# Linear attention into a Swish layer: fewer idle products at the start, beta copied earlier, batch 2's numerators moved

## The chip, the cores and the metric

The kernel runs on one core of a Trainium2 chip. Its five engines work side by side, each through its own queue of instructions in order: PE (TensorE, matrix products; its weight loads are listed as PEld), DVE (VectorE), ACT (ScalarE), POOL (GpSimd) and SP (SyncE, which here issues DMAs only). They wait for one another through semaphores. The metric is device time in microseconds (us), the median of the runs. Line numbers (L254) are those of the kernel before.

## The reference

Inputs: q, k, v of shape 8 x 8 x 576 x 64 (batch, heads, positions, head size), w_in 512 x 2048, w_out 2048 x 512, beta 2048, all float32.

```python
def phi(x): return np.where(x > 0, x, np.exp(x) - 1.0) + 1.0
q_p, k_p = phi(q), phi(k)
kv  = np.einsum('bhsd,bhse->bhde', k_p, v)
z   = np.sum(k_p, axis=2)
num = np.einsum('bhsd,bhde->bhse', q_p, kv)
den = np.einsum('bhsd,bhd->bhs', q_p, z)[..., None] + 1e-06
x   = num / den          # then to (8*576) x 512, heads side by side
h   = x @ w_in
g   = h * (1.0 / (1.0 + np.exp(-beta * h)))
out = g @ w_out
```

So each batch goes through a small attention part (phi, kv, z, numerators) and then through two large products, of 512 by 2048 and back.

## The kernel before, in words

Everything is written in the order in which it is to be queued; nothing is rearranged later, so the order of the lines is the order of work on each engine. Large data is bf16, sums are float32 in PSUM.

**Tiling.** A batch has 576 positions: four blocks of 128 and a tail of 64, called t = 0 to 4. The tails of all batches are collected in xT_tail and done as a ninth batch at the end. The two big products of a batch are h_phase (16 groups, one for each ff, of four products 128 x 128 by 512; `h_mm`, L331, then Silu on ACT) and y_phase (four tiles y of sixteen products; `y_mm`, L349, then `y_out`). The attention part of batch b + 1 is put between these groups: `at(sh, n, f)` runs f behind group n of h_phase, `at(sy, n, f)` behind group n of y_phase. Their instructions go into the same PE queue, so a product that must wait holds all groups behind it.

**Start.** For batch 0 there is no other work to hide in. `idle(n)` (L130) queues n products that nobody reads. Then come, on PE: the transposes of phi_q (`q_trans`, L254, 16 of them into two PSUM tiles tps), three idle products, z's products (L187) of head pair 0, six idle products, z's of pair 1, kv's products of pair 0 (`kv_direct`), the denominators (`dens`, L411), two groups of numerators of pair 0 (`numer_part`, L490), kv's of pair 1. phi itself is an exponential on ACT (`phi_part`, L141), a relu on DVE (`phi_relu`, L145, called r) and a minimum of both on DVE (`phi_min`, L152). Of kv, pair 0 goes from PSUM into kv0 by two masked DVE operations, pair 1 by four casts on ACT (L543), which numer_part(..., 1) needs. beta is loaded as a row, turned by one product into bps (L538) and copied by ACT into beta_s (L546). The numerators, divided, are xs; `x_part(t, pr)` transposes a half of xs on PE (L511) and copies it with ACT (L515) into xT, and `h0_part` (L521) makes the first h products, block by block.

The PSUM tiles of `q_trans`, bps and x_part share a pool of two buffers, in turn: a tile waits until the tile two places before it has been read. bps and x_part(0, 0) take the two buffers, so x_part(1, 0) waits for the copy of bps.

**Batch 2 inside batch 1.** During h_phase of batch 1: phi_q of batch 2 is transposed by two DMAs issued on SP, `q_trans_dma` (L265), one for each half of the partitions, into qTd; `kv_both` (L176) stands behind group 6; x_trans(1, 4) behind group 8; and `numer(2, t)` (L282) behind groups 9, 11, 13, 15 and 16, that is, the first group of y_phase for the last one. A numer makes four products, two with the first half of qTd and two with the second, then three DVE operations (L290, L291, L296). Its PSUM tile has a pool of one buffer. One group later `x_trans_dma` (L323) transposes the xs by a DMA on SP. For the later batches the numerators lie behind groups 5, 7, 9, 11 and 13.

phi_q of batch 2 is worked on DVE behind the last copies of xT and y_sb of the phase before. v of batch 2 comes through POOL's DMA queue and is copied by POOL itself into vaug (`v_copy`, L166). The loads of q and k for batch 3 wait for qTd by an explicit dependency (`hold`).

Of the kernel before, what the change touches and what calls it, by code (L numbers as in the profile page):

```python
# [8 lines left out]
F32 = mybir.dt.float32  # L9
# [7 lines left out]
def kernel(  # L17
# [10 lines left out]
    nc = tc.nc  # L28
# [4 lines left out]
    P = 128  # L33
    KC = DM // P
    FC = DFF // P
# [10 lines left out]
    miscps = ctx.enter_context(tc.tile_pool(name="miscps", bufs=2, space=bass.MemoryType.PSUM))  # L46
# [44 lines left out]
    beta_row = consts.tile([FC, P], F32)  # L91
# [10 lines left out]
    ident16 = consts.tile([FC, FC], F32)  # L102
# [25 lines left out]
    def idle(n, cols=512):  # L128
        for _ in range(n):
            nc.tensor.matmul(  # L130
                warm_ps[:, 0:cols], warm[:, 0:P], warm[:, 0:cols], start=True, stop=True
            )
# [31 lines left out]
    def v_copy(eng, b, pr):  # L164
        src = vb[b % 2] if b == 2 else vf[b % 2]
        eng.tensor_copy(  # L166
            vaug[b % 2][:, pr, :, :, 0:D],
            src[:, 2 * pr : 2 * pr + 2].rearrange("p h j d -> p j h d"),
        )
# [13 lines left out]
    def row_products(b, pr, dsts, mov):  # L183
        for j in range(J):
            for hh in range(2):
                r = slice(hh * G, (hh + 1) * G)
                nc.tensor.matmul(  # L187
                    dsts[hh], st[b, "k"][r, pr, j, :], mov(r, j),
                    start=(j == 0), stop=(j == J - 1), skip_group_check=True,
                )  # L190

    def z_products(b, pr, ps):

        row_products(b, pr, [a[:, 256 + 2 * pr : 258 + 2 * pr] for a in ps], lambda r, j: ones[r])

    def z_evac(ps):
        for hh in range(2):
            nc.vector.tensor_mul(
                z0[:, hh], ps[hh][:, 256:260].rearrange("p (a h) -> p a h", a=2),
                kvmask[:, :, :, 0],  # L200
            )

    def kv_direct(b, pr, ps):
        row_products(
            b, pr, [a[:, pr * P : (pr + 1) * P].rearrange("p (h d) -> p h d", h=2) for a in ps],
            lambda r, j: vb[b][r, 2 * pr : 2 * pr + 2, j, :],
        )
# [53 lines left out]
    def q_trans_dma(b):  # L261
        st[b, "qTd"] = work.tile([P, 38, G], BF16, tag="qT", name="qTd")
        nc.gpsimd.memset(st[b, "qTd"][:, 36:37], 0.0)
        for hh in range(2):
            st[b, "qTd", "dma"] = nc.sync.dma_start_transpose(  # L265
                out=st[b, "qTd"][:, hh * 2 * J : (hh + 1) * 2 * J],
                in_=st[b, "q"][hh * G : (hh + 1) * G].rearrange("p a j c -> p (a j c)"),
            )

    def q_stat(b, t, hh, pr, n):  # L270
        if (b, "qTd") in st:
            i = (hh * 2 + pr) * J + 2 * t
            return st[b, "qTd"][:, i : i + 2, :].rearrange("p j g -> p (j g)")
        return st[b, "qT"][:, t, pr, hh, 0:n]
# [32 lines left out]
    def x_trans(b, t, eng):  # L307
        n = P if t < NT - 1 else G
        xv = st[b, "xs", t].rearrange("p i a d -> p (i a d)")
        tp = miscps.tile([P, KC, P], BF16, tag="misc", name="xtp")  # L310
        for p in range(KC):
            nc.tensor.matmul(  # L312
                tp[:, p, :n], xv[:n, p * P : (p + 1) * P], identity[:n, :n],
                is_transpose=True, start=True, stop=True, skip_group_check=True,
            )
        if eng is nc.scalar:
            nc.scalar.copy(x_dst(b, t), tp[:, :, :n])
        else:
            eng.tensor_copy(x_dst(b, t), tp[:, :, :n])  # L319
# [23 lines left out]
    def mm_tile(name):  # L343
        return mmps.tile([P, 512], F32, tag="mm", name=name)
# [45 lines left out]
    beta_s = consts.tile([P, FC], F32)  # L390
# [10 lines left out]
    def misc_bf():  # L401
        return miscps.tile([P, 1024], BF16, tag="misc", name="tp")
# [18 lines left out]
    def num0_tile():  # L421
        return num0ps.tile([P, 512], F32, tag="num0", name="nps0")
# [16 lines left out]
    def phi_step(a, pr, f, *r):  # L439
        f(0, a, pr, *((xin(0, a, pr),) if f is not phi_min else ()), *r)  # L440
# [5 lines left out]
    phi_step("q", 0, phi_part)  # L446
    phi_step("q", 1, phi_part, 0, 4)
    phi_step("q", 1, phi_part, 4, J)
    idle(20)
    phi_step("q", 0, phi_relu)  # L450
    phi_step("q", 0, phi_min)
    phi_step("q", 1, phi_relu)
# [24 lines left out]
    z_products(0, 0, zt)  # L477
    idle(6)
    z_products(0, 1, zt)
    z_evac(zt)  # L480

    def q_trans0(t):
# [2 lines left out]
    def numer_part(ts, pr):  # L485

        nps = num0_tile()
        for i, t in enumerate(ts):
            for hh in range(2):
                nc.tensor.matmul(  # L490
                    nps[:, (i * 2 + hh) * P : (i * 2 + hh + 1) * P].rearrange(
                        "p (h d) -> p h d", h=2
                    ),
                    q_stat(0, t, hh, pr, P),
                    st[0, "kv"][:, hh, pr, :].rearrange("p (h e) -> p h e", h=2)[:, :, 0:D],
                    start=True, stop=True, skip_group_check=True,
                )
        for i, t in enumerate(ts):
            if pr == 0:
                st[0, "xs", t] = work.tile([P, 4, 2, D], BF16, tag="xs", name="xs", bufs=4)  # L500
            nc.vector.tensor_mul(  # L501
                st[0, "xs", t][:, 2 * pr : 2 * pr + 2].rearrange("p i a d -> p a i d"),
                nps[:, i * 256 : (i + 1) * 256].rearrange("p (a h d) -> p a h d", a=2, h=2),
                rden0[:, t, :, 2 * pr : 2 * pr + 2, None].to_broadcast([P, 2, 2, D]),
            )

    def x_part(t, pr):
        xv = st[0, "xs", t].rearrange("p i a d -> p (i a d)")
        tp = misc_bf()[:, 0:256].rearrange("p (c t) -> p c t", c=2)
        for c in range(2):  # L510
            nc.tensor.matmul(  # L511
                tp[:, c], xv[:, (2 * pr + c) * P : (2 * pr + c + 1) * P], identity,
                is_transpose=True, start=True, stop=True, skip_group_check=True,
            )
        nc.scalar.copy(xT[0][:, 2 * pr : 2 * pr + 2, t * P : (t + 1) * P], tp)  # L515

    def h0_part(t, pr, ffs=range(4)):

        for ff in ffs:
            for kc in range(2 * pr, 2 * pr + 2):  # L520
                nc.tensor.matmul(  # L521
                    hps[ff][:, t * P : (t + 1) * P],
                    w_in_sb[0][:, kc, ff * P : (ff + 1) * P],
                    xT[0][:, kc, t * P : (t + 1) * P],
                    start=(t == 0 and kc == 0), stop=(t == 3 and kc == KC - 1),
                    skip_group_check=True,
                )
# [6 lines left out]
    numer_part((0, 1), 0)  # L534
    numer_part((2, 3), 0)
    kv_direct(0, 1, kvp0)
    bps = miscps.tile([P, FC], F32, tag="misc", name="bps")
    nc.tensor.matmul(bps, beta_row, ident16, is_transpose=True, start=True, stop=True)  # L538

    for hh in range(2):  # L540
        for h in range(2):
            r = slice(h * D, (h + 1) * D)
            nc.scalar.copy(  # L543
                kv0[r, hh, 1, h * EA : h * EA + D], kvp0[hh][r, P + h * D : P + (h + 1) * D]
            )
    nc.scalar.copy(beta_s, bps)  # L546
    hps = [mm_tile("h_ps") for _ in range(4)]
    x_part(0, 0)
    x_part(1, 0)
    numer_part((0, 1), 1)  # L550
    h0_part(0, 0)
    x_part(2, 0)
    h0_part(1, 0)
    x_part(3, 0)
# [138 lines left out]
    def at(side, n, *fs):  # L693
        side.setdefault(n, []).extend(fs)


    for b in range(1, B + 1):
        n = b + 1
        sh, sy = {}, {}
        if b == 1:  # L700
            at(sh, 0, lambda: q_trans_dma(2))
            at(sh, 8, lambda: x_trans(1, 4, nc.vector))
            at(sh, 1, lambda: [v_copy(nc.gpsimd, 2, pr) for pr in range(2)])
            at(sh, 2, lambda: load_kq(3, st[2, "qTd", "dma"]), lambda: load_v(3))
        if n < B:
            at(sh, 6 if b == 1 else 4, lambda: kv_both(n))
            for t in range(NT):
                ff = min((9 if b == 1 else 5) + 2 * t, FC)
                for g, f in ((ff, numer), (ff + 1, x_trans_dma)):
                    at(*((sh, g) if g < FC else (sy, g - FC)), lambda t=t, f=f: f(n, t))  # L710
        if n + 1 < B:
            m = n + 1
            at(sy, 0, lambda: phi_all(m, "q"))
            at(sy, 2, lambda: q_trans_dma(m), lambda: load_kq(m + 1, st[m, "qTd", "dma"]))
            at(sy, 6, lambda: phi_all(m, "k"), lambda: [v_copy(nc.gpsimd, m, pr) for pr in range(2)])
            at(sy, 7, lambda: load_v(m + 1))
        h_phase(b, xT[b % 3] if b < B else xT_tail, sh)
        y_phase(b, sy, last=(b == B))
# [30 lines left out]
```

## Time and profile before

| | us |
|---|---|
| median of 3 runs (294.74 to 295.0) | 294.87 |
| the profiled execution, its own time | 295.34 |
| its span, first to last instruction | 293.6 |
| PE busy | 286.4 |
| ACT busy | 160.2 |
| DVE busy | 115.9 |
| first h product of 512 columns (L331) starts | 21.19 |
| h_phase of batch 1 starts | 52.68 |

Times in the profile count from the start of the span. Timelines have one line for a run of like instructions: start, length, engine, line, operation, what it writes and reads, how many, and in brackets the idle time before it on its engine and what ended it. The chain of waits is the work that ended last, followed back from the end: each piece is what the next one waited for. An end of a PE product is modelled, so starts are the safer numbers.

The granted clock of TensorE reads 1.00 in every stretch.

### The profile page before, as it was taken

What the parts mean: (1) busy time and instruction counts of PE and PEld (TensorE: products, weight loads), DVE (VectorE), ACT (ScalarE), POOL (GpSimd) and SP (SyncE); (2) the same over time, 40 slices, a digit from 0 to 9 for tenths busy, and PEclk for the clock granted to TensorE, in tenths of its full rate; (3) what the DMA queues carried; (4) which work ended last, traced back from release to release, by engine and by line L of the source; (5) the groups of instructions that cost most, each with busy time, mean ns of one, the idle gap of its engine ahead of it and who ended that gap; (6) DMA issues with size and microseconds to landing.
All of it is one profiled execution on the core that took longest, in us unless ns stands there. A gap on an engine that the chain in (4) does not pass through costs nothing.

```text
span 293.6 us, 4773 instructions
## 1 busy us (share of the span) xinstructions
PE 286.4 (98%) x1890; PEld 143.8 (49%) x1890; DVE 115.9 (39%) x267; ACT 160.2 (55%) x217; POOL 36.9 (13%) x54
## 2 busy tenths in 40 slices
PE   8989999999999999999999999999999999999994
PEld 2674457454445444544455445544554444444443
DVE  5742776843815461446135613562251200110021
ACT  5677757957635862677267815790660077017500
POOL 8632100220050005000500053000000000000000
PEclk9999999999999999999999999999999999999999
DMA  8999999699799859953997399728132310130032
GB/s 217 206 227 387 261 232 178 129 224 189 94 166 286 132 71 194 281 86 55 181 285 107 44 197 264 116 42 157 38 72 45 74 36 0 43 84 18 0 74 73
DMA packets 50887, 40.83 MB, mean 139 GB/s; under 512 B 30752, under 2 KB 42288, under 8 KB 50864
## 3 DMA queue, kind: packets, MB, share of 16 engines
q1 hardware_dynamic: 37968, 23.48, 37.9%
q0 software_dynamic: 12736, 16.91, 30.0%
q8 instruction: 15, 0.25, 0.3%
q10 hardware_dynamic: 160, 0.13, 0.2%
q14 instruction: 8, 0.07, 0.1%
HBM read 36.71 MB, written 9.44 MB: 157 GB/s over the span
## 4 chain that ended last, share of the span: by engine, by line
PE 96%; DVE 2%; ACT 1%; issue 0%; DVEq 0%
PE y_ps L349 42%; PE h_ps L331 42%; PE warm_ps L130 3%; PE nps L282 2%; PE kvp L176 2%; PE h_ps L521 1%; PE kv L187 1%; PE xtp L312 0%; PE nps L429 0%; PE nps L254 0%; PE tp L511 0%; PE nps L411 0%; DVE xs L501 0%; DVE phi_k L152 0%; DVE xs L296 0%
## 5 line engine op out<-in xcount | busy, mean ns | idle before, releaser
L339 ACT ACTIVATE g<-h_ps,beta_c 128x512 bf16<-128x512 f32 x144 | 98.0, 688 | 100.5 <-PE h_ps L331 100.0
L349 PE MATMUL y_ps<-w_out,g 128*128 128x512 bf16 (+3 forms) x600 | 127.2, 370 | 0.0
L331 PE MATMUL h_ps<-xT,w_in 128*128 128x512 bf16 x496 | 114.7, 379 | 0.3 <-DVE xT L319 0.2
L349 PEld LDWEIGHTS <-g 128*128 128x128 bf16 x600 | 58.0, 98 | 64.7
L331 PEld LDWEIGHTS <-w_in 128*128 128x128 bf16 x560 | 52.7, 98 | 57.8 <-issue 0.2
L234 DVE COPY y_sb<-y_ps 128x512 f32<-128x512 f32 (+2 forms) x35 | 23.4, 673 | 84.7 <-PE y_ps L349 81.0
L296 DVE TENSOR_TENSOR xs<-nps,rden 128x512 bf16<-128x512 f32 (+1 forms) x36 | 24.7, 689 | 5.9 <-DMA xT<-xs 3.5
L82 POOL DMA_DIRECT2D xq<-in_q_dram x7 | 5.2, 744 | 109.6 <-DMA qTd<-phi_q 105.9
L141 ACT ACTIVATE e<-xk 128x1152 bf16<-128x1152 bf16 x16 | 17.9, 1153 | 1.0 <-DMA xk<-in_k_dram 0.9
L152 DVE TENSOR_TENSOR phi_q<-e,r 128x1152 bf16<-128x1152 bf16 (+2 forms) x17 | 12.0, 720 | 14.0 <-ACT e L141 13.7
L141 ACT ACTIVATE e<-xq 128x1152 bf16<-128x1152 bf16 x14 | 15.6, 1156 | 0.1
L331 PE MATMUL h_ps<-xT_tail,w_in 128*128 128x512 bf16 x64 | 14.0, 379 | 0.0
L226 DVE TENSOR_TENSOR kv_bd<-kvp,kvmask 128x260 bf16<-128x260 f32 x12 | 4.6, 423 | 23.7 <-PE kvp L176 23.7
L290 DVE TENSOR_SCALAR den<-nps 128x8 f32<-128x8 f32 (+1 forms) x30 | 4.9, 165 | 22.7 <-PE nps L282 22.7
L282 PEld LDWEIGHTS <-qTd 128*128 128x128 bf16 x120 | 9.3, 98 | 7.7 <-DVE xs L296 0.9
L152 DVE TENSOR_TENSOR phi_k<-e,r 128x1152 bf16<-128x1152 bf16 x16 | 11.6, 753 | 2.2 <-ACT e L141 2.0
L282 PE MATMUL nps<-kv_bd,qTd 128*128 128x130 bf16 x120 | 11.9, 221 | 0.4 <-DVE xs L296 0.4
L166 POOL CAST vaug<-vf 128x1152 bf16<-128x1152 f32 x10 | 11.2, 1157 | 5.1 <-DMA vf<-in_v_dram 5.1
L130 PE MATMUL warm_ps<-xT 128*128 128x512 bf16 x29 | 9.7, 500 | 1.5 <-DVE xT L95 1.5
L141 ACT ACT_TABLE_LOAD x6 | 7.7, 1283 | 2.0 <-DMA xq<-in_q_dram 1.2
L339 ACT ACT_TABLE_LOAD x6 | 7.7, 1283 | 0.1
L176 PEld LDWEIGHTS <-phi_k 64*128 64x128 bf16 x216 | 6.3, 94 | 2.5 <-issue 2.1
(81 smaller groups left out, 122.1 us busy)
## 6 DMA issues: line engine op xcount, KB each, us to landing
out_dram<-y_sb SPq DMA_DIRECT2D x70, 128.0 KB, 2.4
vf<-in_v_dram SPq DMA_DIRECT2D x5, 1152.0 KB, 10.2
xk<-in_k_dram POOLq DMA_DIRECT2D x7, 576.0 KB, 13.9
xq<-in_q_dram POOLq DMA_DIRECT2D x7, 576.0 KB, 8.9
w_in<-in_moe_w_in_dram POOLq DMA_DIRECT2D x4, 512.0 KB, 12.4
g<-in_moe_w_out_dram POOLq DMA_DIRECT2D x2, 1024.0 KB, 18.3
stage<-in_moe_w_out_dram POOLq DMA_DIRECT2D x2, 1024.0 KB, 21.0
stage<-in_q_dram SPq DMA_DIRECT2D x2, 576.0 KB, 4.2
```

What stands on the lines that cost most here:

```text
L82: return eng.dma_start(out=dst[:, h0 : h0 + n].rearrange("p h j d -> p h (j d)"), in_=rows.rearrange("(i p) e -> p i e", p=P)[:, h0 : h0 + n],
L130: nc.tensor.matmul(warm_ps[:, 0:cols], warm[:, 0:P], warm[:, 0:cols], start=True, stop=True)
L141: nc.scalar.activation(st[b, a, pr, "e"][:, :, j0:j1], x[:, :, j0:j1], ACTF.Exp)
L152: nc.vector.tensor_tensor(st[b, a][:, pr, j0:j1].rearrange("p j (h d) -> p j h d", h=2), st[b, a, pr, "e"][:, :, j0:j1].rearrange("p h j d ...
L166: eng.tensor_copy(vaug[b % 2][:, pr, :, :, 0:D], src[:, 2 * pr : 2 * pr + 2].rearrange("p h j d -> p j h d"),)
L176: nc.tensor.matmul(ps[hh, pr], st[b, "k"][r, pr, j, :], vaug[b % 2][r, pr, j, :, 0:EA], start=(j == 0), stop=(j == J - 1), skip_group_chec ...
L234: eng.tensor_copy(dst, src)
L282: nc.tensor.matmul(nps[: qs.shape[-1], hh, pr * 2 * EA : (pr + 1) * 2 * EA], qs, st[b, "kv"][:, hh, pr, :], start=True, stop=True, skip_gr ...
L296: nc.vector.tensor_mul(xs[:n].rearrange("p i a d -> p a i d"), num, rd[:, :, :, None].to_broadcast([n, 2, 4, D]),)
L331: nc.tensor.matmul(hp[:, c0:c1], w_in_sb[ff // 4][:, kc, (ff % 4) * P : (ff % 4 + 1) * P], x[:, kc, c0:c1], start=(kc == 0), stop=(kc == K ...
L339: nc.scalar.activation(g_sb[b % 2][:, ff, :], hp, ACTF.Silu, scale=beta_c[:, ff : ff + 1])
L349: nc.tensor.matmul(yp[:, c0:c1], g_sb[b % 2][:, ff, t * P : (t + 1) * P], w_out_sb[i][:, c, c0:c1], start=(ff == 0), stop=(ff == FC - 1), ...
```

## The change

Three places change. The first `idle` makes 15 products, not 20. The beta product and its ACT copy come before z_evac and kv's products instead of behind them. ACT's casts of kv's pair 1 are taken apart: the two of the first half (`diagonal(0)`), then the copy of x_part(0, 0), then the two of the second half; and h0_part(0, 0) comes ahead of numer_part((0, 1), 1). On PE, bps now takes the first buffer of the pool of two before x_part does. For batch 2 the numerators lie behind groups 8, 10, 12 and 14 of h_phase and, as before, the first of y_phase; the DMA transposes one group behind each.

```diff
-    idle(20)
+    idle(15)
...
     z_products(0, 1, zt)
+    bps = miscps.tile([P, FC], F32, tag="misc", name="bps")
+    nc.tensor.matmul(bps, beta_row, ident16, is_transpose=True, start=True, stop=True)
+    nc.scalar.copy(beta_s, bps)
     z_evac(zt)
...
     kv_direct(0, 1, kvp0)
-    bps = miscps.tile([P, FC], F32, tag="misc", name="bps")
-    nc.tensor.matmul(bps, beta_row, ident16, is_transpose=True, start=True, stop=True)
-
-    for hh in range(2):
+
+    def diagonal(hh):
+
         for h in range(2):
             r = slice(h * D, (h + 1) * D)
             nc.scalar.copy(
                 kv0[r, hh, 1, h * EA : h * EA + D], kvp0[hh][r, P + h * D : P + (h + 1) * D]
             )
-    nc.scalar.copy(beta_s, bps)
+
+    diagonal(0)
+    x_part(0, 0)
+    diagonal(1)
     hps = [mm_tile("h_ps") for _ in range(4)]
-    x_part(0, 0)
     x_part(1, 0)
+    h0_part(0, 0)
     numer_part((0, 1), 1)
-    h0_part(0, 0)
     x_part(2, 0)
...
-                ff = min((9 if b == 1 else 5) + 2 * t, FC)
+                ff = (8 if b == 1 else 5) + 2 * t
                 for g, f in ((ff, numer), (ff + 1, x_trans_dma)):
```

## The prediction

> **What bounds the kernel now.** I read the totals first, then the chain of waits from the start, then the timelines of the two places that the change touches. TensorE (PE) is busy for nearly the whole span, so a change pays only where PE waits, or where it does work that only fills time:
>
> ```profile
> PE 286.4 (98%) x1890; PEld 143.8 (49%) x1890; DVE 115.9 (39%) x267; ACT 160.2 (55%) x217; POOL 36.9 (13%) x54
> ```
>
> The chain of waits, in order of time (start, length, what), shows the start-up as a relay between engines:
>
> ```profile
> 1.46 7.39 PE warm_ps L130 x20
> 8.85 0.46 PE tp L254 x8
> ...
> 9.68 0.76 DVE phi_k L152
> ...
> 10.48 0.38 PE nps L187 x18
> 10.86 1.40 PE warm_ps L130 x6
> ...
> 15.76 0.18 ACT beta_s L546
> ...
> 15.99 0.27 PE tp L511 x2
> ```
>
> Idle products hold q's transposes; behind those wait the qT copy, phi_k, z's products. Later PE waits for ACT's beta copy, a wait that the list of waits gives 0.8 us. After 21.19 PE hardly rests until the numerators of batch 2, where the timeline has:
>
> ```profile
> 62.69 0.43 PEld L282 LDWEIGHTS <-qTd 128*128 128x128 bf16 x4
> 62.90 0.40 PE L282 MATMUL nps<-kv_bd,qTd 128*128 128x130 bf16 x4
> ...
> 70.40 0.41 PE L282 MATMUL nps<-kv_bd,qTd 128*128 128x130 bf16 x4 [0.36 <-DVE xs L296]
> ```
>
> The first group does not wait; the last one waits 0.36 us for the one PSUM buffer.
>
> **Part 1, five idle products fewer.** In the timeline of weight loads those of L130 lie 0.427 us apart up to 6.98 and 0.215 from 7.39 on: 14 products at the long pace, 6 at the short one. The granted clock reads 1.00 throughout, so the spacing is what tells. The five removed are of the short pace: 5 x 0.215 = 1.08 us. q's transposes could start at 8.85 - 1.08 = 7.77. phi_q is there: its two last pieces (7.21, 0.43 and 0.48 long) end at about 7.64 and 8.04, and the second eight transposes start at 7.77 + 0.46 = 8.23. Not all of 1.08 arrives. DVE is in k's relu (7.96 to 8.43), so the qT copy, 9.33 now, starts at about 8.34 and the next instruction 0.35 later, at 8.69; but the first exponential of k ends on ACT at 7.57 + 1.16 = 8.73, so phi_k starts at 8.76 instead of 9.68. That is 0.92 us, and z's first products come at 9.56. The six idle products then run to 9.56 + 0.38 + 1.40 = 11.34 (12.26 now). k's second half is no new wait: its exponential ends at 8.96 + 1.16 = 10.12, phi_k by 10.90. **-0.92.**
>
> **Part 2, beta and the first copy of x.** The beta product now stands ahead of kv's products. Its start-to-next is 14.77 to 14.93, 0.16 us, and there it is on the path: -0.76 remains. Its buffer is free (qT copy over by 10.2), beta_row landed at 1.75 + 5.3 = 7.05, and ACT is idle from 12.60, so the copy itself costs nothing. kv's last product ends at 14.84 - 0.76 = 14.08. Now ACT does four casts (0.87), beta_s (0.18), then x's copies, and PE reaches its first h products at 16.49, after x(1,0)'s transposes and one numerator group. Afterwards: two casts to 14.54, a copy of 0.37 to 14.91, h0_part(0,0) at 14.95; two casts to 15.34, the numerators at 15.40; the second copy to 15.72, h0_part(1,0) at 15.78 instead of 17.04. From there the order is the old one: **-1.26 in all at 21.19**, bounds -0.9 (nine steps of the relay, each 0.04 us later) and -1.35 (PE without a gap). In the forecast below this size hardly counts, since a fixed time takes its place. w_in's first quarter has landed: POOL's issue of 14.69 was released by it.
>
> Loads fixed by their own queue leave room for this: k of batch 1 lands at 34.28, its phi is done at 38.6, z's products come at 40.3; v lands at 20.59 + 21.8 = 42.4, is used at 43.7; q and k of batch 2 land at 45.3 and 48.1, wanted at 47.0 and 49.6. One thing moves against a fixed time, in part 3.
>
> **Part 3, numerators of batch 2 one group sooner.** Gain: the last group no longer follows its neighbour by one group, so the 0.36 goes. Cost: the first group comes before the h products of ff 9, 4 x 0.216 = 0.87 earlier, and its third product reads the second half of qTd:
>
> ```profile
> 56.35 3.57 SPq L265 DMA_TRANSPOSE qTd<-phi_q  x2
> ```
>
> and in the list of DMA issues, in the stretch of the second one alone (the last figure is us to landing):
>
> ```profile
> qTd<-phi_q SPq DMA_TRANSPOSE x1, 4.8
> ```
>
> The second transpose is issued at 57.76 (the first takes 1.40) and lands 4.8 later, 62.56. PE's third weight load at 62.89 did not wait, so it had landed by then: 62.56 to 62.89. The third product, 63.01 now, would come at 62.14 on the old clock, so it waits 0.42 to 0.75, and some 0.1 more for a load that nothing covers. Nothing else stands in PE's queue that could run. If all had moved by 1.26 alike, the sum were -1.26 - 0.36 + (0.52 to 0.85) = -1.10 to -0.77.
>
> But qTd hangs on DVE: phi_q of batch 2 begins with the relu at 53.74, and DVE works without a break from 52.20, released by PE. Moved by 1.26 the relu stands at 52.48, and there POOL is copying v, at a time that v's landing fixes (29.46 + 21.5 = 50.96):
>
> ```profile
> 50.99 2.23 POOL L166 COPY vaug<-vf 128x1152 bf16<-128x1152 bf16 x2 [20.47 <-DMA vf<-in_v_dram]
> ...
> 53.74 0.45 DVE L145 TENSOR_SCALAR r<-xq 128x1152 bf16<-128x1152 bf16 x1
> ```
>
> Now that copy lies beside instructions that read PSUM, and none is longer for it (two y_sb copies of 0.68, the mean of all 35 is 0.67). What SBUF-to-SBUF work costs beside POOL, one place shows:
>
> ```profile
> 29.83 0.61 DVE L593 TENSOR_SCALAR w_out<-g,rbeta 128x512 bf16<-128x512 f32 x1
> ...
> 30.20 0.32 POOL L263 MEMSET qTd<- 128x64 bf16 x1
> ...
> 30.36 0.47 DVE L593 TENSOR_SCALAR w_out<-g,rbeta 128x512 bf16<-128x512 f32 x1
> ```
>
> The memset is 0.16 elsewhere and the scale 0.47: each lost about 0.15, nearly the memset's length. So I bound the relu's wait between 0 and the rest of POOL's second copy, 53.22 - 52.48 = 0.74, and take 0.74, as the only pair of this kind held fully. The chain to qTd then gains 0.52, not 1.26: the third product waits 1.16 to 1.49, plus 0.1. **Sum: -1.26 - 0.36 + (1.26 to 1.59) = -0.36 to -0.03, -0.2 taken.** k's phi is later alike, and its products' wait (some 0.15) lies inside the longer one.
>
> On this the Trainium skill, "SBUF — State Buffer", section "Who interferes with whom", says that VectorE in a two-port mode, which a tensor_scalar can enter, and GpSimd exclude one another for a whole instruction, whoever comes first. If only the row's own 0.15 were lost, the sum would be -0.8; the rule's whole instruction makes it -0.2. No row here shows a relu beside a POOL copy.
>
> Moved steps that cost nothing: the four transposes of xs for x^T are issued on SP up to 0.87 sooner on the old clock, past no other DMA; the xs that waits for one of them (3.14 us before 74.38) holds y's copy at 77.06, whose buffer PE wants only at 83.6.
>
> **The rivals.**
> - *No port wait.* The relu runs beside POOL's copy; the memset speaks against it, the PSUM copies for it. -0.95: 293.9.
> - *The start gains little.* If PE's pace rises sooner in the timed runs than at 7.4, phi_q and not the idle products holds q's transposes, and part 1 gives nothing: 0.3 to 0.5 from part 2. Then the relu hardly meets POOL and the sum is -0.4 - 0.36 + 0.68 = -0.1: 294.8. The three times within 0.26 us speak for a steady start.
> - *The pace falls back: slower.* The fifteen products leave one behind the rise. If PE drops to 0.427 at h0_part and needs again the 5.98 us that 14 products took, it does 2.99 us of work in them and loses 2.99: the start is +1.7 late, the relu misses POOL's copy, +1.7 - 0.36 + 0.68 = +2.0: 296.9. It decides from a loss of about 1.5 us, 3 us at the long pace. Against it: 0.77 us of rest at 15.2 changed no pace in this profile.
>
> "TensorE: Matmul & The Clock Gate" (its Parts 1 and 4) speaks for this third rival: the clock is released by free-running windows of activity, about 3.4 us, in which transposes do not count as other products do. The rise here, 5.9 us after the first product, fits such windows; how few products would be too few, no row of this profile shows.
>
> **How the numbers follow.** The profiled execution took 295.34 us, span 293.6 and 1.74 around it, 0.47 above the median of 294.87. -0.2 makes it 295.1; against the median that is 294.65, the forecast. About 0.2%, 0.59 us, is what can be told from no change. Chances: port wait 0.60 (of it faster 0.09, same 0.48, slower 0.03, from qTd's landing times of 4.1 to 5.6), no port wait 0.22 (faster 0.20), small start gain 0.08 (same 0.07, faster 0.01), pace lost 0.10 (slower). Together faster 0.30, same 0.57, slower 0.13. The range must reach the second case with some of its spread, 293.6, and above takes qTd's slower landing, 295.1; the lost pace stays out. The likeliest case alone: 294.4 to 294.95.
>
> **What would show it.** Right: first L331 product near 19.9, no PE wait at beta_s; the relu of q, batch 2, at 53.2 and not at 52.5; PE idle about 1.2 us before the third L282 product, released by a DMA; no wait at the last L282 group. Wrong: idle loads 0.427 apart after 7.5, a relu that starts inside POOL's copy, a qTd that is ready when PE comes, or PE waiting on w_in near 14.9.

## The result, and the profile after

The changed kernel takes 294.75 us (median of 4, 294.35 to 295.15), beside 294.81 for the kernel before in the same runs: ratio 0.9998, 95% interval 0.998 to 1.0016. No difference can be told, as forecast (294.65). The profiled execution took 295.02 us with a span of 293.1, against 295.34 and 293.6. The cause that I gave for it, POOL holding batch 2's relu, is not what happened. The start gained 0.38 us where I had 1.26, and so the relu came too late to be held by POOL. That the time came out right is luck: a start gain that was too large and a wait that did not come nearly cancel.

The chain of waits of the changed kernel, in order of time (start, length, what):

```profile
1.24 6.94 DMA xk<-in_k_dram
...
8.20 1.17 ACT e L141
...
9.40 0.77 DVE phi_k L152
...
10.21 0.38 PE nps L187 x18
...
12.30 0.16 PE bps L481
12.46 0.61 PE kvp L187 x18
...
15.30 0.38 ACT xT L518
...
15.72 0.61 PE h_ps L524 x8
```

The idle products ahead of q's transposes have left the chain (the six between z's halves, 10.59 to 11.99, are still in it); it begins with the load of k. Its first half landed at 8.18 here; in the profile before, ACT could start on it at 7.57. (L481 is the beta product, L518 x's copy and L524 h0_part in the new numbering.) The list of what PE waited for says the same:

```profile
PE nps L187 <- DVE phi_k L152: 1.1, 1, 1.1
PE tp L254 <- DVE phi_q L152: 0.9, 1, 0.9
PE h_ps L524 <- ACT xT L518: 0.3, 1, 0.3
PE nps L282 <- DMA qTd<-phi_q: 0.3, 1, 0.3
```

The wait for beta (0.8) and that for the last numerators (0.4) are gone. In their place PE waits for phi_q, for phi_k, for x's copy and for qTd. The timeline at batch 2:

```profile
51.27 2.23 POOL L166 COPY vaug<-vf 128x1152 bf16<-128x1152 bf16 x2 [21.11 <-DMA vf<-in_v_dram]
...
53.36 0.45 DVE L145 TENSOR_SCALAR r<-xq 128x1152 bf16<-128x1152 bf16 x1
...
61.65 0.29 PE L282 MATMUL nps<-kv_bd,qTd 128*128 128x130 bf16 x2
...
62.24 0.29 PE L282 MATMUL nps<-kv_bd,qTd 128*128 128x130 bf16 x2 [0.29 <-DMA qTd<-phi_q]
...
69.97 0.40 PE L282 MATMUL nps<-kv_bd,qTd 128*128 128x130 bf16 x4
```

The relu keeps its 0.45: POOL's copy is all but over (51.27 + 2.23 = 53.50). The group of four products is torn in two by qTd, and the last group no longer waits.

### The profile page after: what moved, and what is told of

Read it like the earlier page. It is cut to its first block, busy times and chain, and to the rows that moved or that the text cites. A ratio compares the mean times of both kernels' runs of the same rounds, so it can differ in the third digit from the quotient of the medians.

```text
span 293.1 us, 4762 instructions
## 1 busy us (share of the span) xinstructions
PE 284.6 (97%) x1885; PEld 143.0 (49%) x1885; DVE 116.2 (40%) x267; ACT 160.0 (55%) x217; POOL 36.9 (13%) x54
## 4 chain that ended last, share of the span: by engine, by line
PE 93%; DMA 4%; ACT 1%; DVE 1%; issue 0%; SPq 0%; POOLq 0%
PE y_ps L349 43%; PE h_ps L331 40%; PE nps L282 2%; DMA xk<-in_k_dram 2%; PE kvp L176 2%; DMA qTd<-phi_q 2%; PE h_ps L524 1%; PE kv L187 1%; PE warm_ps L130 0%; PE nps L429 0%; PE kvp L187 0%; ACT e L141 0%; PE xtp L312 0%; PE nps L493 0%; PE nps L254 0%
## 5 line engine op out<-in xcount | busy, mean ns | idle before, releaser
L331 PE MATMUL h_ps<-xT,w_in 128*128 128x512 bf16 x496 | 114.7, 379 | 0.3 <-DVE xT L319 0.2
L331 PEld LDWEIGHTS <-w_in 128*128 128x128 bf16 x560 | 52.7, 97 | 57.8 <-issue 0.2
L331 PE MATMUL h_ps<-xT_tail,w_in 128*128 128x512 bf16 x64 | 14.0, 379 | 0.0
L282 PEld LDWEIGHTS <-qTd 128*128 128x128 bf16 x120 | 9.3, 98 | 7.4 <-DMA qTd<-phi_q 0.5
L282 PE MATMUL nps<-kv_bd,qTd 128*128 128x130 bf16 x120 | 12.1, 221 | 0.3 <-DMA qTd<-phi_q 0.3
L130 PE MATMUL warm_ps<-xT 128*128 128x512 bf16 x24 | 7.4, 465 | 1.5 <-DVE xT L95 1.5
```

The source lines that it names most:

```text
L130: nc.tensor.matmul(warm_ps[:, 0:cols], warm[:, 0:P], warm[:, 0:cols], start=True, stop=True)
L282: nc.tensor.matmul(nps[: qs.shape[-1], hh, pr * 2 * EA : (pr + 1) * 2 * EA], qs, st[b, "kv"][:, hh, pr, :], start=True, stop=True, skip_gr ...
L331: nc.tensor.matmul(hp[:, c0:c1], w_in_sb[ff // 4][:, kc, (ff % 4) * P : (ff % 4 + 1) * P], x[:, kc, c0:c1], start=(kc == 0), stop=(kc == K ...
```

## A ruler for the experiments

The times of one kernel spread by 1 us, more than most of the effects. The profiles are steadier if they are cut at marks, so for each I give: when k's first exponential starts on ACT (k has landed), when z's first products start (z), when the first product of L331 starts (h), and when batch 2's h_phase starts (h2).

| profile of | idle products | k | z | z - k | h | h - z | h2 - h |
|---|---|---|---|---|---|---|---|
| before | 20 | 7.57 | 10.48 | 2.91 | 21.19 | 10.71 | 62.41 |
| after | 15 | 8.20 | 10.21 | 2.01 | 20.81 | 10.60 | 62.34 |
| e1_idle15 | 15 | 7.97 | 9.98 | 2.01 | 20.68 | 10.70 | 62.41 |
| e2_beta | 20 | 8.20 | 10.21 | 2.01 | 20.81 | 10.60 | 62.41 |
| e3_numer8 | 20 | 7.76 | 9.77 | 2.01 | 20.48 | 10.71 | 62.35 |
| e4_numer9_last17 | 20 | 7.61 | 10.11 | 2.50 | 20.82 | 10.71 | 61.87 |
| e5_after_last17 | 15 | 7.81 | 9.82 | 2.01 | 20.42 | 10.60 | 61.88 |
| e6_vcopy_twice | 15 | 8.07 | 10.08 | 2.01 | 20.68 | 10.60 | 64.16 |
| e7_idle8 | 8 | 8.20 | 10.21 | 2.01 | 21.51 | 11.30 | 62.36 |
| e8_beta_in_dps | 15 | 7.94 | 9.95 | 2.01 | 20.30 | 10.35 | 61.87 |
| e9_idle4 | 15 | 8.13 | 10.14 | 2.01 | 20.21 | 10.07 | 61.87 |
| e10_idle4_tail19 | 15 | 7.67 | 9.68 | 2.01 | 19.72 | 10.04 | 62.41 |
| e11_dps_tail19 | 15 | 7.95 | 9.96 | 2.01 | 20.32 | 10.36 | 61.87 |

Each edit has its own column: the idle products z - k, beta h - z, the numerators h2 - h. The column k belongs to no edit; it is the luck of the loads, 7.57 to 8.20. Each row is one execution.

## The experiments

**The three edits one by one.** First the idle products alone:

```diff
-    idle(20)
+    idle(15)
```

> Only the first edit: 15 idle products, all else as before. Idle-products theory (they hold q's transposes): z's first products come 0.92 us after-before earlier, 295.34's own clock 10.48 to 9.56, all later work of the start 0.92 earlier; the relu of q, batch 2, would then meet POOL's copy, and the first numerators, behind group 9 as before, have 0.87 more room, so the whole is 0.5 to 0.9 shorter: 293.9 to 294.3. Load theory (phi_q and the landing of k's first half hold the start, the pace of PE rises at a time of its own in each execution): z's first products follow k's exponential by 2.0 us as in the profile of the changed kernel, PE sits idle before q's transposes or before z, and the median moves by less than 0.3 us.

Measured: 294.51 us, ratio 0.9992 (0.9983 to 1.0); z 2.01 after k. The load theory holds for z: with 15 products it never came at any other distance. With 20 it came 2.91, 2.50 and twice 2.01 after k. Which of them it is, the weight loads of the idle products tell: their pace rose at about 7.4 in the profile before, 6.6 in that of e4, 4.9 and 5.7 in those of e2 and e3. So the five products cost 0.9, 0.5, 0 and 0 us: something only where the pace rises late. The profile I forecast from was the one with the latest rise and the earliest k.

The second edit alone (beta's product and copy ahead, the casts taken apart, h0_part(0, 0) ahead of the numerators; 20 idle products, old numerators):

> Only the second edit: beta's product and copy ahead of kv's, x's first copy between the casts, h0_part(0,0) ahead of the numerators; 20 idle products and the numerators as before. Both theories expect the same sum of rows: beta's product costs 0.16 us ahead of kv's, the wait of 0.77 us for its copy goes, from the end of kv's last product to the first of L331 6.2 to 6.0 us in place of 6.5, the whole 0.3 to 0.5 shorter: 294.4 to 294.6. If the beta copy was only the last of several waits, less than 0.15 is left.

Measured: 294.69 us, ratio 0.9999 (0.999 to 1.0008). h - z is 10.60 in place of 10.71: 0.11 gained, not 0.34. That is in the range that I had put for beta's copy being only the last of several waits. But from the casts on 0.36 is gained; the product of beta, ahead of kv's, takes 0.25 of it back (e8, and part 2 below).

The third edit alone:

```diff
-                ff = min((9 if b == 1 else 5) + 2 * t, FC)
+                ff = (8 if b == 1 else 5) + 2 * t
```

> Only the third edit: batch 2's numerators behind groups 8, 10, 12, 14 and the first of the y products. Transpose theory: the third product of the first group waits for the second half of qTd by 0.3 to 0.75 us, the wait of 0.36 before the last group goes, the sum is -0.1 to +0.4: 294.8 to 295.3. If qTd is there in time (the landing of 4.8 us was of that execution alone), no wait and -0.36: 294.5.

Measured: 294.9 us, ratio 1.0002 (0.9994 to 1.0011). PE waits 0.31 at the third product, and h2 - h is 62.35: 0.06 gained. The next run keeps the room between the groups and gives up the earlier start:

```diff
-                ff = min((9 if b == 1 else 5) + 2 * t, FC)
+                ff = (9 if b == 1 else 5) + 2 * t
```

> A form of the third edit that does not need qTd sooner: groups 9, 11, 13, 15 and the second of the y products for the last, so two apart everywhere and none sooner. Transpose theory: no wait at the first group, no wait of 0.36 at the last: 0.36 shorter than before, 294.5, and 0.3 to 0.4 shorter than the form with group 8. If the wait at the last group was only room for a later wait, the time stays at 294.8.

Measured: 294.62 us, ratio 1.0006 (0.9994 to 1.0018), its times from 294.17 to 296.08. In the profile h2 - h is 61.87: 0.54 shorter than before, 0.48 shorter than with group 8. So the wait at the last group was worth 0.54, and the wait for qTd costs 0.48: nearly all of it back. The median does not show the 0.54; the last experiments suggest a reason.

**The better numerators in the changed kernel.** Its third edit is replaced by that of e4.

> The changed kernel with batch 2's numerators behind groups 9, 11, 13, 15 and the second of the y products. Transpose theory: neither the wait for qTd (0.47 from the first h product to batch 2's h_phase, as the profiles give it) nor the wait before the last group (0.54): from the first product of L331 to batch 2's h_phase 61.87 us as in the run with that form alone, 0.47 less than in the changed kernel; the median 294.2 to 294.4. If the gain of that run belonged to its own execution, 62.3 and 294.75.

Measured: 294.24 us, ratio 0.9982 (0.9969 to 0.9996), h2 - h 61.88. So the gain shows in a second profile, and here in the median too: 0.68 under the kernel before in the same runs.

**Do POOL and the relu shut one another out?** In the changed kernel they hardly met, so this run makes them:

```diff
-            at(sh, 1, lambda: [v_copy(nc.gpsimd, 2, pr) for pr in range(2)])
+            at(sh, 1, lambda: [v_copy(nc.gpsimd, 2, pr) for pr in (0, 1, 0, 1)])
```

> The changed kernel with POOL's copy of batch 2's v made twice over, the same values into the same places, so that POOL copies from about 51.3 to 55.7, beside the first relu and the first minimum of batch 2. Port theory (as in the prediction): the relu, alone 0.45, waits for the copy that is running, up to 1.1 us, or the copies get longer than 1.15; phi_q and with it qTd come 0.7 to 3 us later and PE waits that much longer before the third product of the first numerators. No-port theory: relu 0.45, minimum 0.76, the copies 1.15 each, all as without.

One execution: 296.7 us. Its timeline:

```profile
50.95 4.63 POOL L166 COPY vaug<-vf 128x1152 bf16<-128x1152 bf16 x4 [20.53 <-DMA vf<-in_v_dram]
...
53.23 1.35 DVE L145 TENSOR_SCALAR r<-xq 128x1152 bf16<-128x1152 bf16 x1
54.68 1.50 DVE L152 TENSOR_TENSOR phi_q<-e,r 128x1152 bf16<-128x1152 bf16 x1
...
63.92 0.29 PE L282 MATMUL nps<-kv_bd,qTd 128*128 128x130 bf16 x2 [1.00 <-DMA qTd<-phi_q]
```

The relu takes 1.35 and not 0.45, the minimum 1.50 and not 0.76, POOL's four copies 1.16 each as always. DVE loses 0.90 and 0.74, and h2 - h grows by 1.82: 0.7 more at the third product, 0.9 before kv's. The port theory holds: DVE came second and was held, for most of a copy. This agrees with what the prediction cites of the Trainium skill, "SBUF — State Buffer", section "Who interferes with whom". By the whole-instruction rule with copies 1.16 apart from 50.95, the third ends at 54.43, 1.20 after 53.23, and the relu would take 0.45 more, 1.65; it took 1.35, so it was held for 0.3 less than that. These durations cannot tell a full hold from a strong slowing, and spans on POOL are rough in a profile.

**How few idle products are too few?**

```diff
-    idle(15)
+    idle(8)
```

> The changed kernel with 8 idle products in place of 15, so that they end at about 4.9 and PE has nothing to do until phi_q. Load theory: z's first products come 2.0 us after k's first exponential starts, as with 15, and the time stays at 294.6 to 294.9 if PE's pace has risen by then. Pace theory (third rival): the weight loads of the transposes and of kv's products lie at the long pace, h products of 128 columns 0.11 apart and not 0.056, the whole 1 to 3 us longer.

Measured: 296.08 us, ratio 1.0034 (1.0024 to 1.0044). z keeps its 2.01, as the load theory says, but h - z grows from 10.60 to 11.30. The answer by stretches (busy time and count of each engine, then the granted clock, the share of the DMA engines, GB/s):

```profile
7.50:8.50 1.00, 0.84 (x15) 0.85 (x16) 0.80 (x3) 0.30 (x1) 1.00 (x2) 1.00 1.18 199
8.50:10.30 1.80, 1.42 (x12) 0.28 (x10) 1.40 (x4) 1.56 (x2) 1.64 (x3) 0.51 1.20 205
10.30:12.60 2.30, 2.30 (x24) 0.91 (x24) 1.26 (x3) 2.28 (x4) 1.28 (x2) 0.64 1.23 206
12.60:16.00 3.40, 3.35 (x84) 2.64 (x84) 2.29 (x10) 1.18 (x6) 1.45 (x2) 1.00 1.24 207
```

After 2.3 us of rest, in two pieces, and the transposes the granted clock falls to 0.51, and comes back within 10.3 to 12.6. That is the third rival, in a kernel with 8 products: 0.70 us in this profile; the median is 1.16 above that of the kernel before in the same runs. The forecast had written +2.0 for it. With 15 no profile shows it.

**Beta where PE waits anyway.** e5, and beta's product further up, ahead of the three idle products:

```diff
+    bps = dps[:, 256 : 256 + FC]
+    nc.tensor.matmul(
+        bps, beta_row, ident16, is_transpose=True, start=True, stop=True, skip_group_check=True
+    )
+    nc.scalar.copy(beta_s, bps)
     nc.scalar.activation(tiny[:, 1:2], warm[:, 0:1], ACTF.Silu)
     idle(3)
...
     z_products(0, 1, zt)
-    bps = miscps.tile([P, FC], F32, tag="misc", name="bps")
-    nc.tensor.matmul(bps, beta_row, ident16, is_transpose=True, start=True, stop=True)
-    nc.scalar.copy(beta_s, bps)
```

> As the run with groups 9 to 15 and the second y product, and beta's product moved further up, ahead of the three idle products, into a free part of the denominators' PSUM tile, its copy ahead of ACT's table load. There PE waits for phi_k in most profiles, so the 0.24 that the product costs ahead of kv's should go: from z's first products to the first of L331 10.36 us in place of 10.60, the median 294.0 to 294.2. If the casts, not kv's products, hold the first h products, 10.5 to 10.6 and no gain.

h - z is 10.35, 0.25 less than in e5, so beta's product had cost that. The median, 294.41 (0.9984, 0.9973 to 0.9995), does not show it beside e5's 294.24. Then two idle products fewer between z's halves:

```diff
-    idle(6)
+    idle(4)
     z_products(0, 1, zt)
```

> The run with beta's product in the denominators' tile, and besides 4 idle products between z's two halves in place of 6. In all profiles the second half of phi_k is ready 0.4 to 0.5 us before those six end, so two fewer take 0.4 off: from z's first products to the first of L331 9.95 us in place of 10.35, if PE keeps the short pace; the median 293.7 to 293.9. The start then is early enough for batch 2's relu of q to meet POOL's second copy: it should last 0.5 to 0.9 in place of 0.45, and with the numerators behind group 9 PE still not wait for qTd. If the pace falls back as with 8 idle products, some of the later products lie 0.427 apart and the time is 294.5 or more.

Measured: 294.31 us, ratio 0.9989 (0.9975 to 1.0002), times from 293.61 to 295.88. h - z fell to 10.07, 0.28 of the 0.4, since phi_k's second half (ready at 11.51) now holds z's. The relu met POOL as expected, 0.77 in place of 0.45. But PE had a wait that I had not named, in batch 2's h_phase:

```profile
84.73 0.69 DVE L234 COPY y_sb<-y_ps 128x512 f32<-128x512 f32 x1 [4.96 <-DMA out_dram<-y_sb]
...
85.48 1.89 PE L331 MATMUL h_ps<-xT,w_in 128*128 128x512 bf16 x8 [0.64 <-DVE y_sb L234]
```

PE wants the PSUM buffer of batch 1's last y. Its copy waits for a y_sb buffer, that for a store, and the stores stand on SP behind the transposes of batch 3's q, which stand behind the transpose of batch 2's tail. With the last numerators one group later, DVE does the tail's xs behind phi_q of batch 3, 1.0 us after it, and q's transposes wait on SP for the tail's. The order is the same in e8, whose profile shows no wait; but in e9 batch 3's q also landed later, so that its relu starts at 70.54 and not at 69.57. So the last two runs move the tail's transpose one group on, behind the fourth group of y (the first expectation below says third):

```diff
-                for g, f in ((ff, numer), (ff + 1, x_trans_dma)):
+                for g, f in ((ff, numer), (ff + (2 if ff > FC else 1), x_trans_dma)):
```

> The run with 4 idle products between z's halves, and the DMA transpose of batch 2's tail one group later (behind the third of the y products), so that on SP it comes behind the two transposes of batch 3's q and no longer holds them. Queue theory: in the run before, PE waited 0.64 us in batch 2's h_phase for a y_sb copy, that for a store of y, that for SP's transposes of batch 3's q, which stood behind the tail's transpose until its xs was done, 1.1 us after phi_q of batch 3. Without it those transposes start when phi_q is done, stores and copy come some 1 us sooner, PE's wait of 0.64 goes: the median 293.5 to 293.8. If the wait hangs on the loads of batch 3 and not on that order, it stays at 0.5 or more and the time at 294.2 to 294.4.

> The run with beta's product in the denominators' tile, with six idle products, and the same later transpose of the tail. Queue theory: its profile showed no wait for y_sb, with 0.4 us of room; executions with a late landing used that room up, so the median goes from 294.4 to 294.0 to 294.2 and the highest times (294.8 to 295.2) go. Against the form with 4 idle products it is 0.3 to 0.4 longer. If the order on SP does nothing, the times stay as they were.

Measured: e10 293.84 us, ratio 0.9964 (0.9952 to 0.9976); e11, with the six idle products, 293.77, ratio 0.9966 (0.9954 to 0.9978). Beside the kernel before, 294.75 in the same runs, e10 is 0.91 us faster and e11 0.98; e10 gained a little less than expected, e11 more. The changed kernel was not among these runs; no difference from the kernel before could be told for it. The wait for y_sb is gone, and so are the high times: e11's lie within 293.72 to 293.92. SP's queue, first in e8, then in e11:

```profile
74.96 1.17 SPq L323 DMA_TRANSPOSE xT_tail<-xs  x1
76.22 3.59 SPq L265 DMA_TRANSPOSE qTd<-phi_q  x2
```

```profile
74.03 3.46 SPq L265 DMA_TRANSPOSE qTd<-phi_q  x2
77.58 2.04 SPq L364 DMA_DIRECT2D out_dram<-y_sb  x2
```

q's transposes start 2.2 us sooner. The queue theory holds for e9. That it is also what spread the times of e4, e5 and e8 fits, but is argued only: of these profiles only e4's shows a loss there, of 0.07. What they do show is that hardly any room was left. From the end of that y_sb copy to the product that needs its buffer it is 0.12 in e5 and 0.21 in e8, and 0.06 in e4 and e9, where PE waited; in e10 and e11 it is 1.7. q's landing alone moved by 1.0 between e8 and e9.

e10 was expected 0.3 to 0.4 below e11 and is not. Its start is the earliest of all, 19.72, 0.60 ahead of e11's, and there the forecast's own mechanism takes it back:

```profile
51.05 2.23 POOL L166 COPY vaug<-vf 128x1152 bf16<-128x1152 bf16 x2 [20.41 <-DMA vf<-in_v_dram]
...
52.43 1.17 DVE L145 TENSOR_SCALAR r<-xq 128x1152 bf16<-128x1152 bf16 x1
```

The relu, 0.85 before the end of POOL's copy, takes 0.72 longer; h2 - h is 62.41 in place of 61.87, and 0.54 of the 0.60 are gone. Most of it goes ahead of the second half of kv's products, where PE waits for phi_k (0.17 idle, some 0.36 from start to start); at the third product of the first numerators, for qTd, it is about 0.18. The forecast had put the wait for phi_k at nothing, as lying inside a longer one.

## Why the prediction was right, and where it was wrong

- **The verdict, 294.65 against 294.75, was right by luck; the case that I named as the likeliest was not the one that came.** It was closer to the second rival, "the start gains little", at 294.8. I had given that 0.08.
- **Part 1, -0.92: wrong as a forecast for the median.** The step that failed is taking the pace of PE and the landing of k from one execution. For that execution the working was right: z - k was 2.91, and 2.01 with 15 products, a gain of 0.90. But 2.01 was also reached with 20 products in two profiles of four, and k's landing alone moves z by up to 0.63. In the profile after, the pace rose at 5.1, as the second rival supposes, and k's later landing took 0.63 of the 0.90. I had read the three times within 0.26 us as a steady start; with more runs the kernel before spreads from 294.23 to 295.43.
- **Part 2, -0.34: right mechanism, two steps wrong.** Beta's product costs 0.25 and not 0.16 ahead of kv's (e8). I had counted from its own start, 14.77, to the next; but the product before it starts at 14.62, and in that row products lie 0.05 apart, so 0.1 goes ahead of it. And I set a start against a time of the chain. In the profile before, the chain and the timeline have the same products, h0_part(1, 0) with the two transposes ahead of them, as

```profile
16.93 0.11 PE tp L511 x2
17.04 0.45 PE h_ps L521 x8
```

```profile
16.77 0.27 PE L511 MATMUL tp<-identity,xs 128*128 128x128 bf16 x2
16.88 0.61 PE L521 MATMUL h_ps<-xT,w_in 128*128 128x128 bf16 x8
```

The chain's times (first fence) are modelled ends put one behind the other, here 0.16 later than the starts (second fence). My 15.78 was a start, and the old one is 16.88, not 17.04. From the first cast (14.87 less 0.76, so 14.11) to these products I had 1.67 us for the new kernel; it is 1.66 (14.85 to 16.51). Before it was 2.01, not 2.17, so 0.35 was to be gained and not 0.50; to the first product of L331 it is 6.32 before and 5.96 after, 0.36.

- **Part 3, qTd: right.** Without POOL I had 0.52 to 0.85 with the uncovered load; it is 0.48 (e3 against e4), just under. The gain at the last group was undersized: 0.54, not 0.36. The idle time of 0.36 counts from the modelled end of the product before; from start to start the two lie 0.74 apart (69.67 to 70.40), where in a full queue it is 0.215, so the stop cost 0.52. So the sum of part 3 is -0.06 in place of +0.16 to +0.49.
- **The port wait: right as a mechanism, not met here.** The relu came at 53.36 and not 52.48, since the start gained 0.38 and not 1.26. Where the start is as early as I had written, the relu is held: from 52.43 by 0.72 in e10, where I had 0.74 from 52.48. The upper bound, the rest of POOL's copy, was the right end to take. In that run, with the first numerators behind group 9, it cost 0.54 in time.
- **The third rival** did not come with 15 idle products and came with 8 (e7); nothing between was run.
- What I said would show the forecast wrong did: the relu starts inside POOL's copy, at 53.36, and keeps its 0.45. The signs of its being right failed too: the first L331 product is at 20.81, not near 19.9, and PE is idle 0.29 before the third product of L282, not 1.2. Two held: no wait for beta_s, and none at the last group.

## What to carry to other kernels

Before a gain at the start is taken from one profile, ask which of its terms are the kernel's and which are that execution's: the landing of the first loads and the rise of PE's pace moved by 0.6 and 3 us between profiles of like kernels, and distances between marks that an edit did not touch held to 0.02. When a stage is moved earlier, list the events that stay where they are (loads, and what other engines do when those land): each is the next place where the gain can end, as POOL's copy and SP's order of transposes were here. Here a wait that was taken away by moving its consumer sooner came back as the wait for another producer; giving the groups room without starting sooner kept the whole 0.54 in the profiles. And take both ends of a difference from one kind of view: starts with starts, not starts with the chain's times.

## What the runs showed of the hardware that was not expected

- PE's pace rises at a time of its own: from loads 0.427 us apart to 0.215 anywhere from about 4.4 (e9) to 7.4 (before), with the first product at 1.46 each time. The granted clock reads 1.00 through all of that start, but 0.51 in e7 after a rest of 2.3 us.
- A product of 16 x 16 in float32 cost 0.25 us in PE's queue ahead of kv's products (e5 against e8), a little more than one bf16 product of 512 columns at the short pace (0.215).
- A relu of 0.45 us on DVE, with input and output in SBUF, takes longer when POOL is copying SBUF to SBUF: by 0.32 with 0.46 of the copy to go (e9), by 0.72 with 0.85 (e10), by 0.90 with 1.20 (e6), by nothing with 0.14 (after). In these four it lost the rest of the copy, less 0.13 to 0.3.
